# Spectral mixing and gated MLP on one core: the first eight chunks of the first matmul stage in another order, with the first four row norms on VectorE

## The chip, the cores and the metric

One core of a Trainium2 chip runs the whole kernel. Its engines are named as in the profile: PE (TensorE, matmuls), PEld (its weight loads), DVE (VectorE), ACT (ScalarE), POOL (GpSimd) and SP (SyncE, which here only issues DMAs). Each engine takes its own instructions strictly in the order in which the program gives them and waits on semaphores of the others. The metric is the device time of one execution in microseconds (us), as the median of several runs. A lower number is better.

## What is computed

The part that matters is the first block, an adaptive layer norm followed by a Fourier mixing over the sequence (2048 positions) and the hidden axis (512):

```python
sa, ca, ga, sb, cb, gb = (mod[:, 0], mod[:, 1], mod[:, 2], mod[:, 3], mod[:, 4], mod[:, 5])
h = _layernorm(x, axis=-1) * (1 + ca) + sa
a = jnp.einsum("bsd,ed->bse", h, dft_hid_re)
b = jnp.einsum("bsd,ed->bse", h, dft_hid_im)
y = jnp.einsum("ts,bse->bte", dft_seq_re, a) - jnp.einsum("ts,bse->bte", dft_seq_im, b)
x = x + ga * y
```

After it come a second layer norm, a gelu layer, a second sequence mixing with `w_sp`, a gate and an output projection. They are the other nine tenths of the time, and the change touches nothing in them.

## The kernel before

The sequence product is taken first, on the normalised rows, and the hidden transform later. Every float32 product is made of three matmuls on a high and a low part of each operand: high by high, high by low, low by high. The high part is a rounded copy (on ACT, line 249, or DVE, line 247), and the low part is the rest (a DVE subtraction, line 256).

**Rows.** `x` is cut into 16 row tiles of 128 positions. Row tile s is normed into `xn` (its column 0 is set to 1, a place for the mean), copied into a high part `hh` (line 416, ACT), and the rest goes into a low part `hl` (line 421, DVE). For rows 0 to 3 `stats_first` makes mean and variance on DVE (lines 374 to 377), then POOL raises the variance to the power -1/2 (line 378) and multiplies it with the negated mean (line 379). ACT then applies scale and shift (line 119). Rows 4 to 9 go the same way by `stats_x` and `norm` (lines 103 to 115), with three small POOL instructions each (lines 107, 108, 115) and a POOL memset of column 0 (line 402).

**Chunks.** The DFT matrices are loaded in blocks of 512 by 512 (1 MB, four DMAs of 256 KB each) into `stage`, a pool of two buffers. One chunk n is a quarter of a block, turned by a DVE transpose into `t` (line 176 for one chunk, line 220 for two), split into `ah` and `al`, and used in 12 matmuls: four column groups of the row tile, three products each. Below, "chunk n" is that group of 12 matmuls, "ah n" and "al n" its operands, and "row s" the row tile. `ah` has four buffers, `al` three, and `t` two buffers of two chunks each.

In the first output tile (t = 0) the real and imaginary products collect in PSUM banks 0 to 3 and 4 to 7. Before the change chunks 0 to 3 are the four quarters of real block 0 with rows 0 to 3, chunks 4 to 7 the four quarters of imaginary block 1 with the same rows, chunks 8 to 11 real block 2 with rows 4 to 7, chunks 12 to 15 imaginary block 3 with rows 4 to 7, and so on.

**Order.** Nothing is scheduled by a tool: the order on each engine is the order of the code. For each n the loop calls `prep(n)` (low part of chunk n + 2, transpose of chunks n + 4 and n + 5, high part of chunk n + 3), then `mm_a(n)` (the matmuls), then `run(n)`, which issues what `at(n, ...)` has put down for this place. The work before chunk 0 is written out by hand. A DMA issue waits, besides its buffer, for the DMA that was issued eight places earlier to land.

Of the kernel before, what the change touches and what calls it, by code (L numbers as in the profile page):

```python
# [13 lines left out]
P = 128  # L14
# [5 lines left out]
def fnet_gmlp_kernel(  # L20
# [181 lines left out]
    def turn_one(n):  # L202
        squares(slot(n), stage[n // 4], n % 4)
# [167 lines left out]
    def stats_first(s):  # L371

        m = spool.tile([P, 12], F32, tag="first", bufs=4, name=f"first{s}")
        nc.vector.bn_stats(m[:, :6], X[s])
        mv = m[:, 8:]
        nc.vector.bn_aggr(mv[:, :2], m[:, :6])
        nc.vector.tensor_scalar(mv[:, 1:2], mv[:, 1:2], EPS, None, op0=ALU.add)
        nc.gpsimd.tensor_tensor(mv[:, 2:3], mv[:, 1:2], mhalf, op=ALU.pow)
        nc.gpsimd.tensor_scalar(mv[:, 3:4], mv[:, 0:1], mv[:, 2:3], -1.0, op0=ALU.mult, op1=ALU.mult)
        NRM[s] = mv[:, 2:3], mv[:, 3:4]  # L380
# [48 lines left out]
    def mm_a(n):  # L429
        t, r = divmod(n, 8 * NQ)  # L430
        j, s = ((r // 4) % 2, r // 8 * 4 + r % 4) if t == 0 else (r // NS, r % NS)
# [5 lines left out]
        if n < 4:  # L437
            order = (h_hi[s], al), (h_lo[s], ah)
            for a, b in ((h_hi[s], ah),) + (order if n else order[::-1]):
                for k in range(ND):  # L440
                    nc.tensor.matmul(GP[0, 0, k], a[:, k, :], b, start=s == 0 and b is ah and a is h_hi[s], stop=False)
            return
# [505 lines left out]
    for s, n in ((4, 4), (5, 4), (6, 6), (7, 6), (8, 10), (9, 10)):  # L948
# [242 lines left out]
```

## Time and profile before

| | |
|---|---|
| median of 3 runs | 949.35 us (948.96 to 949.91) |
| profiled execution, whole | 948.98 us |
| profiled execution, span of the instructions | 947.2 us |
| PE busy | 940.0 us, 99% of the span |
| DVE busy | 704.0 us, 74% |
| ACT busy | 388.4 us, 41% |
| POOL busy | 174.3 us, 18% |
| PE share of the chain that ended last | 95% |

The profiled execution takes 1.8 us more than the span, which lies outside the instructions. PE is busy all the time but for 7.2 us, so a change shows in the time only where PE starts earlier, waits less, or waits more. PE's waits are listed by who ended them; the timeline then tells when each of them was and what came late.

### The profile page before, as it was taken

The page shows a single profiled execution, that of the slowest core. Times are in us where ns is not written, and L with a number is a line of the kernel's source. Part 1 is how long each engine was busy: PE and PEld are TensorE (multiplying, and loading weights), DVE is VectorE, ACT ScalarE, POOL GpSimd, SP SyncE. Part 2 cuts the span into 40 slices and gives each one's busy share as a digit, 9 for nine tenths or more (in the row PEclk, how much of TensorE's full clock was granted, in tenths as well). Part 3 has the DMA queues.
Part 4 walks back from the last instruction along what each step waited for, and adds up shares of the span by engine and source line. Part 5 has one row for each costly group of instructions (what it writes and reads, how often), then busy time and mean ns, then how long its engine had stood idle before and what let it go on. Part 6 is the DMA issues. An engine that isn't in the chain of part 4 may idle for free.

```text
span 947.2 us, 12274 instructions
## 1 busy us (share of the span) xinstructions
PE 940.0 (99%) x4160; PEld 781.3 (82%) x4160; DVE 704.0 (74%) x1039; ACT 388.4 (41%) x665; POOL 174.3 (18%) x331
## 2 busy tenths in 40 slices
PE   8999999999999999999999999999999999999998
PEld 5888888888888888888888999888888888888886
DVE  6799857775576667767978588877788688885872
ACT  4685424232132222322776356644544444331221
POOL 2430000221531144122332265200000000000000
PEclk9999999999999999999999999999999999999999
DMA  9996553576437975996397985555554456833541
GB/s 213 222 222 149 113 139 89 147 187 156 134 89 195 274 212 153 279 280 140 126 307 281 327 266 152 155 114 134 128 133 90 105 118 140 206 102 120 192 162 57
DMA packets 249230, 161.25 MB, mean 170 GB/s; under 512 B 130192, under 2 KB 218512, under 8 KB 249040
## 3 DMA queue, kind: packets, MB, share of 16 engines
q1 hardware_dynamic: 235792, 120.75, 52.8%
q0 software_dynamic: 11984, 39.07, 11.3%
q10 hardware_dynamic: 1392, 0.66, 0.3%
q8 instruction: 32, 0.52, 0.2%
q14 instruction: 30, 0.25, 0.1%
HBM read 123.73 MB, written 36.70 MB: 169 GB/s over the span
## 4 chain that ended last, share of the span: by engine, by line
PE 95%; DMA 2%; DVE 1%; ACT 1%; POOL 1%; issue 0%; ACTq 0%; SPq 0%; POOLq 0%; DVEq 0%
PE gp L95 12%; PE gp L96 12%; PE gp L97 12%; PE gw L96 10%; PE gw L97 10%; PE gw L95 10%; PE yp L96 3%; PE yp L95 3%; PE yp L97 3%; PE z2p L97 3%; PE z2p L96 3%; PE z2p L95 3%; PE op L96 3%; PE op L95 3%; PE op L97 3%; PE z1p L95 1%
## 5 line engine op out<-in xcount | busy, mean ns | idle before, releaser
L249 ACT ACTIVATE ah<-t 128x512 fp32r<-128x512 f32 x263 | 164.2, 627 | 306.6 <-PE gp L97 184.9
L256 DVE TENSOR_TENSOR al<-t,ah 128x512 fp32r<-128x512 f32 x264 | 180.1, 685 | 142.7 <-PE gp L96 65.3
L95 PE MATMUL gp<-ah,hh 128*128 128x512 f32 x496 | 192.9, 389 | 0.0
L96 PE MATMUL gp<-al,hh 128*128 128x512 f32 x496 | 192.9, 389 | 0.0
L97 PE MATMUL gp<-ah,hl 128*128 128x512 f32 x496 | 192.9, 389 | 0.0
L97 PE MATMUL gw<-ah,bl 128*128 128x512 f32 x400 | 155.6, 389 | 0.0
L96 PE MATMUL gw<-al,bh 128*128 128x512 f32 x400 | 155.6, 389 | 0.0
L95 PE MATMUL gw<-ah,bh 128*128 128x512 f32 x400 | 155.6, 389 | 0.0
L97 PEld LDWEIGHTS gp<-ah,hl 128*128 128x128 f32 x496 | 93.1, 188 | 19.4
L95 PEld LDWEIGHTS gp<-ah,hh 128*128 128x128 f32 x496 | 93.1, 188 | 19.3
L96 PEld LDWEIGHTS gp<-al,hh 128*128 128x128 f32 x496 | 93.1, 188 | 19.2
L95 PEld LDWEIGHTS gw<-ah,bh 128*128 128x128 f32 x400 | 75.1, 188 | 15.7
L97 PEld LDWEIGHTS gw<-ah,bl 128*128 128x128 f32 x400 | 75.1, 188 | 15.5
L96 PEld LDWEIGHTS gw<-al,bh 128*128 128x128 f32 x400 | 75.1, 188 | 15.5
L220 DVE STREAM_TRANSPOSE t<-stage 128x1024 f32<-128x1024 f32 x64 | 79.2, 1238 | 5.8 <-DMA stage<-in_A_dft_seq_re_dram 5.4
L214 DVE STREAM_TRANSPOSE t<-stage 128x1024 f32<-128x1024 f32 x56 | 69.3, 1238 | 0.0
L761 ACT ACTIVATE bh<-z 128x512 fp32r<-128x512 f32 (+1 forms) x56 | 32.8, 587 | 65.8 <-PE gw L96 65.8
L739 POOL DMA_DIRECT2D s_d<-sj x64 | 35.1, 550 | 110.5 <-DVE sj L731 81.5
L95 PE MATMUL yp<-hth,gh 128*128 128x512 f32 x128 | 49.8, 389 | 0.0
L96 PE MATMUL yp<-htl,gh 128*128 128x512 f32 x128 | 49.8, 389 | 0.0
L97 PE MATMUL yp<-hth,gl 128*128 128x512 f32 x128 | 49.8, 389 | 0.0
L96 PE MATMUL z2p<-wil,ah 128*128 128x448 f32 x128 | 46.7, 365 | 0.0
(204 smaller groups left out, 1419.3 us busy)
## 6 DMA issues: line engine op xcount, KB each, us to landing
stage<-in_A_dft_seq_im_dram SPq DMA_DIRECT2D x64, 256.0 KB, 5.5
sj<-in_B_w_sp_dram SPq DMA_DIRECT2D x32, 512.0 KB, 8.3
s_d<-sj POOLq DMA_DIRECT2D x64, 256.0 KB, 4.3
stage<-s_d SPq DMA_DIRECT2D x128, 128.0 KB, 2.9
stage<-in_A_dft_seq_re_dram SPq DMA_DIRECT2D x60, 256.0 KB, 5.3
stage<-in_B_w_sp_dram SPq DMA_DIRECT2D x96, 128.0 KB, 3.2
stage<-h_d SPq DMA_DIRECT2D x32, 256.0 KB, 6.0
wm<-in_w_mod_dram SPq DMA_DIRECT2D x16, 256.0 KB, 4.8
```

The lines of the kernel that those rows point to most:

```text
L95: nc.tensor.matmul(acc, ah, bh, start=first, stop=False, skip_group_check=go_on)
L96: nc.tensor.matmul(acc, ah, bl, start=False, stop=False, skip_group_check=go_on)
L97: nc.tensor.matmul(acc, al, bh, start=False, stop=last, skip_group_check=go_on)
L214: nc.vector.transpose(t.rearrange("p r (b i) -> p r b i", i=32), st[:, :, :, 16 * k:16 * k + 32])
L220: nc.vector.transpose(t.rearrange("p k (b i) -> p k b i", i=32), st[:, :, 32 * k:32 * k + 64].rearrange("p b (k i) -> p k b i", k=2))
L249: nc.scalar.activation(AH[n], source(n), AF.Copy)
L256: nc.vector.tensor_tensor(AL[n], source(n), AH[n].bitcast(F32), op=ALU.subtract)
L739: nc.gpsimd.dma_start(s_d[m, r, g][b * P:(b + 1) * P, :], a)
L761: nc.scalar.activation(BH[p, k][:, :w], b_of(p, k), AF.Copy)
```

## The change

Five things are changed, all before or in the first chunks:

- Chunks 0 to 7 alternate: an even chunk is a quarter of real block 0, an odd one the same quarter of imaginary block 1, both with the same row. So row s is used by chunks 2s and 2s + 1, where before chunks 0 to 3 used rows 0 to 3. Each of the eight chunks gets its own transpose of 512 columns (`turn_one`). All eight chunks run the matmuls product by product over the four column groups.
- Rows 0 to 3 are normed on DVE by one instruction (subtract the mean, multiply by the power, `norm_first`) and a DVE memset of column 0. POOL keeps the power alone, and ACT loses four norm instructions.
- The first halves of blocks 0 and 1 are loaded ahead of row 1, rows 1, 2 and 3 in loads of their own. Block 2 goes to the buffer `wb` of another pool, which is free at this time, so that it needn't wait for a `stage` buffer. Block 3 is loaded when chunk 7 has been turned.
- Chunk 0 is turned in two halves, and its high part is made in halves by ACT and DVE.
- The order after chunk 0 is written out: `prep(0)` to `prep(4)` are taken out, and what they did stands in a table. Rows 4 and 5, whose statistics stood together at chunk 4, are now made one after the other at chunks 4 and 5 and later.

The diff (empty lines left out):

```diff
--- before.py
+++ after.py
@@ -199,8 +199,15 @@
             T[n], T[n + 1] = t[:, 0, :], t[:, 1, :]
         return T[n]
-    def turn_one(n):
-        squares(slot(n), stage[n // 4], n % 4)
+    def turn_one(n, b0=0, b1=16):
+        if b0 == 0:
+            slot(n)
+        squares(T[n][:, 32 * b0:32 * b1], stage[n % 2][:, b0:b1], n // 2)
+        if n // 2 == 3 and b1 == 16:
+            stage.pop(n % 2)
+            if n % 2:
+                load(3)
     def turn_two(n):
@@ -376,8 +383,7 @@
         nc.vector.bn_aggr(mv[:, :2], m[:, :6])
         nc.vector.tensor_scalar(mv[:, 1:2], mv[:, 1:2], EPS, None, op0=ALU.add)
         nc.gpsimd.tensor_tensor(mv[:, 2:3], mv[:, 1:2], mhalf, op=ALU.pow)
-        nc.gpsimd.tensor_scalar(mv[:, 3:4], mv[:, 0:1], mv[:, 2:3], -1.0, op0=ALU.mult, op1=ALU.mult)
-        NRM[s] = mv[:, 2:3], mv[:, 3:4]
+        NRM[s] = mv[:, 0:1], mv[:, 2:3]
     def sum_x(s):
@@ -428,17 +434,17 @@
     def mm_a(n):
         t, r = divmod(n, 8 * NQ)
-        j, s = ((r // 4) % 2, r // 8 * 4 + r % 4) if t == 0 else (r // NS, r % NS)
+        j, s = (r % 2, r // 2) if n < 8 else ((r // 4) % 2, r // 8 * 4 + r % 4) if t == 0 else (r // NS, r % NS)
         if s == 0:
             for k in range(ND):
                 GP[t, j, k] = bank(4 * j + k if t == 0 else ring[0] % 6, f"gp{t}_{j}_{k}")
                 ring[0] += t > 0
         ah, al = AH.pop(n), AL.pop(n)
-        if n < 4:
+        if n < 8:
             order = (h_hi[s], al), (h_lo[s], ah)
-            for a, b in ((h_hi[s], ah),) + (order if n else order[::-1]):
+            for a, b in ((h_hi[s], ah),) + (order if j == 0 else order[::-1]):
                 for k in range(ND):
-                    nc.tensor.matmul(GP[0, 0, k], a[:, k, :], b, start=s == 0 and b is ah and a is h_hi[s], stop=False)
+                    nc.tensor.matmul(GP[0, j, k], a[:, k, :], b, start=s == 0 and b is ah and a is h_hi[s], stop=False)
             return
         for k in range(ND):
             matmul3(GP[t, j, k], h_hi[s][:, k, :], h_lo[s][:, k, :], ah, al, s == 0, s == NS - 1)
@@ -894,48 +900,69 @@
     both = (nc.sync, nc.scalar)
+    for b in range(2):
+        stage[b] = blocks.tile([P, 16, P], F32, tag="stage", bufs=2, name=f"stage{b}")
     load_x(0, range(1), both)
-    stage[0] = blocks.tile([P, 16, P], F32, tag="stage", bufs=2, name="stage0")
     load_block(stage[0], src[0], 0, P // 2, both)
-    load_x(0, range(1, 2), both)
+    load_block(stage[1], src[1], 0, P // 2, both)
+    load_x(0, range(1, 2))
     nc.scalar.activation(sc, ones[:, :ND], AF.Silu)
-    load_x(0, range(2, 4))
+    load_x(0, range(2, 3))
     load_block(stage[0], src[0], P // 2, P)
-    load(1)
+    load_block(stage[1], src[1], P // 2, P)
+    load_x(0, range(3, 4))
     load_x(1, range(2))
+    stage[2] = spool.tile([P, 16, P], F32, tag="wb", bufs=1, name="stage2")
+    load_block(stage[2], src[2])
     keep_busy(4, 5)
-    for s in range(4):
+    def norm_first(s):
         LN[s] = spool.tile([P, D], F32, tag="xn", bufs=4, name=f"xn{s}")
-        nc.gpsimd.memset(LN[s][:, 0:1], 1.0)
+        m = NRM.pop(s)
+        nc.vector.tensor_scalar(LN[s], X.pop(s), m[0], m[1], op0=ALU.subtract, op1=ALU.mult)
+        nc.vector.memset(LN[s][:, 0:1], 1.0)
+    def hi_half(n, b0, b1, eng=None):
+        if b0 == 0:
+            split_done.add((n, 0))
+            AH[n] = blocks.tile([P, Q], F32R, tag="ah", bufs=4, name=f"ah{n}")
+        c = slice(32 * b0, 32 * b1)
+        if eng:
+            eng.tensor_scalar(AH[n][:, c], T[n][:, c], 1.0, None, op0=ALU.mult)
+        else:
+            nc.scalar.activation(AH[n][:, c], T[n][:, c], AF.Copy)
     stats_first(0)
-    norm_x(0)
+    norm_first(0)
     hi_h(0)
-    turn_one(0)
-    prep_hi(0, nc.vector)
-    stats_first(1)
+    turn_one(0, 0, 8)
+    hi_half(0, 0, 8)
+    turn_one(0, 8, 16)
+    hi_half(0, 8, 16, nc.vector)
+    prep_lo(0)
     lo_h(0)
-    prep_lo(0)
-    norm_x(1)
-    hi_h(1)
     turn_one(1)
     prep_hi(1)
-    stats_first(2)
+    stats_first(1)
     prep_lo(1)
-    lo_h(1)
-    norm_x(2)
-    hi_h(2)
     turn_one(2)
     prep_hi(2)
-    stats_first(3)
-    turn_one(3)
-    prep_hi(3)
-    norm_x(3)
-    hi_h(3)
-    stage.pop(0)
-    load(2)
-    at(0, lo_h, 2)
-    at(0, turn_two, 4)
-    at(1, lo_h, 3)
+    norm_first(1)
+    hi_h(1)
+    prep_lo(2)
+    lo_h(1)
+    prepared.update(range(5))
+    for n, *todo in ((0, (turn_one, 3), (prep_hi, 3), (stats_first, 2), (prep_lo, 3), (turn_one, 4), (prep_hi, 4)),
+                     (1, (norm_first, 2), (hi_h, 2), (prep_lo, 4), (lo_h, 2), (turn_one, 5), (prep_hi, 5)),
+                     (2, (stats_first, 3), (prep_lo, 5), (turn_one, 6), (prep_hi, 6)),
+                     (3, (norm_first, 3), (hi_h, 3), (prep_lo, 6), (lo_h, 3), (turn_one, 7), (prep_hi, 7)),
+                     (4, (prep_lo, 7), (stats_x, 4), (turn_two, 8)),
+                     (5, (norm_x, 4), (hi_h, 4), (lo_h, 4), (stats_x, 5)),
+                     (6, (norm_x, 5), (hi_h, 5), (lo_h, 5))):
+        for f, *a in todo:
+            at(n, f, *a)
     at(0, load_x, 1, range(2, 4))
     at(2, load_row)
     at(9, silu_row)
@@ -945,7 +972,7 @@
     at(12, load_columns, 0)
     at(19, load_ht, 0)
     at(28, load_ht, 1)
-    for s, n in ((4, 4), (5, 4), (6, 6), (7, 6), (8, 10), (9, 10)):
+    for s, n in ((6, 6), (7, 6), (8, 10), (9, 10)):
         m = n + (s == 9)
         at(n, stats_x, s)
         at(m + 1, norm_x, s)
```

At the start DVE's instructions are these before the change, behind the statistics of row 0 (`first` is the statistics tile of a row, `t` a turned chunk; the number behind a name is the row or chunk, the one behind the underscore a running number):

```order
L176 STREAM_TRANSPOSE t0_187<-stage0_137 128x512
L247 TENSOR_SCALAR ah0_189<-t0_187 128x512
L374 BN_STATS first1_191<-x0_132 128x6
L376 BN_AGGR first1_191<-first1_191 128x2
L377 TENSOR_SCALAR first1_191<-first1_191 128x1
L421 TENSOR_TENSOR hl0_197<-xn0_170,hh0_185 128x512
L256 TENSOR_TENSOR al0_199<-t0_187,ah0_189 128x512
L176 STREAM_TRANSPOSE t0_187<-stage0_137 128x512
L374 BN_STATS first2_207<-x0_132 128x6
L376 BN_AGGR first2_207<-first2_207 128x2
L377 TENSOR_SCALAR first2_207<-first2_207 128x1
```

and these after it:

```order
L924 TENSOR_SCALAR xn0_188<-x0_134,first0_183 128x512
L925 MEMSET xn0_188 128x1
L176 STREAM_TRANSPOSE t0_193<-stage0_132 128x256 x2
L933 TENSOR_SCALAR ah0_195<-t0_193 128x256
L263 TENSOR_TENSOR al0_199<-t0_193,ah0_195 128x512
L427 TENSOR_TENSOR hl0_201<-xn0_188,hh0_191 128x512
L176 STREAM_TRANSPOSE t0_193<-stage1_133 128x512
L381 BN_STATS first1_206<-x0_134 128x6
L383 BN_AGGR first1_206<-first1_206 128x2
L384 TENSOR_SCALAR first1_206<-first1_206 128x1
L263 TENSOR_TENSOR al1_211<-t0_193,ah1_204 128x512
L176 STREAM_TRANSPOSE t2_213<-stage0_132 128x512
```

The row's norm (line 924) and memset now stand on DVE, where they stood on ACT and POOL; al0 stands ahead of hl0, and one row's work lies between the transposes of two chunks.

Around chunk 8, DVE has this before the change (`bstx` and `mvx` are the statistics of a row from 4 on; the first row below ends those of row 4, then come rows 5, 6 and 7):

```order
L105 BN_AGGR mvx_357<-bstx_355 128x2
L103 BN_STATS bstx_364<-x1_160 128x6
L105 BN_AGGR mvx_366<-bstx_364 128x2
L256 TENSOR_TENSOR al7_373<-t6_288,ah7_332 128x512
L256 TENSOR_TENSOR al8_400<-t8_330,ah8_375 128x512
L220 STREAM_TRANSPOSE t10_402<-stage2_236 128x1024
L103 BN_STATS bstx_427<-x1_160 128x6
L105 BN_AGGR mvx_429<-bstx_427 128x2
L103 BN_STATS bstx_436<-x1_160 128x6
L105 BN_AGGR mvx_438<-bstx_436 128x2
L256 TENSOR_TENSOR al9_445<-t8_330,ah9_409 128x512
L421 TENSOR_TENSOR hl4_461<-xn4_394,hh4_423 128x512
```

and this after it, again from the end of row 4's statistics on:

```order
L105 BN_AGGR mvx_360<-bstx_358 128x2
L227 STREAM_TRANSPOSE t8_367<-stage2_173 128x1024
L427 TENSOR_TENSOR hl4_393<-xn4_388,hh4_391 128x512
L103 BN_STATS bstx_395<-x1_168 128x6
L105 BN_AGGR mvx_397<-bstx_395 128x2
L263 TENSOR_TENSOR al8_409<-t8_367,ah8_374 128x512
L227 STREAM_TRANSPOSE t10_411<-stage2_173 128x1024
L427 TENSOR_TENSOR hl5_437<-xn5_432,hh5_435 128x512
L103 BN_STATS bstx_439<-x1_168 128x6
L105 BN_AGGR mvx_441<-bstx_439 128x2
L103 BN_STATS bstx_448<-x1_168 128x6
L105 BN_AGGR mvx_450<-bstx_448 128x2
```

The statistics of row 5 stood right behind those of row 4, and hl4 (with hl5 behind it) stood behind al8 and al9. Now hl4 stands ahead of row 5's statistics and of al8, and hl5 ahead of the statistics of rows 6 and 7; al9 is the row behind the last one shown.

ACT has this at the same place before the change:

```order
L249 ACTIVATE ah8_375<-t8_330 128x512
L119 ACTIVATE xn4_394<-x1_160,nmrx_362,rsx_359 128x511
L119 ACTIVATE xn5_397<-x1_160,nmrx_371,rsx_368 128x511
L249 ACTIVATE ah9_409<-t8_330 128x512
L416 ACTIVATE hh4_423<-xn4_394 128x512
L416 ACTIVATE hh5_425<-xn5_397 128x512
```

and this after it:

```order
L256 ACTIVATE ah8_374<-t8_367 128x512
L119 ACTIVATE xn4_388<-x1_168,nmrx_365,rsx_362 128x511
L422 ACTIVATE hh4_391<-xn4_388 128x512
L256 ACTIVATE ah9_418<-t8_367 128x512
L119 ACTIVATE xn5_432<-x1_168,nmrx_402,rsx_399 128x511
L422 ACTIVATE hh5_435<-xn5_432 128x512
```

The norms of rows 4 and 5 (line 119) stood together; now the copy hh4 and ah9 stand between them.

## Rows read from the trace of the kernel before

**Rows 1.** The page, part 1: busy time of each engine.

```profile
PE 940.0 (99%) x4160; PEld 781.3 (82%) x4160; DVE 704.0 (74%) x1039; ACT 388.4 (41%) x665; POOL 174.3 (18%) x331
```

**Rows 2.** Waits of PE over the span: us in total, times, longest.

```profile
PE gp L441 <- ACT ah L249: 1.1, 2, 0.7
PE z1p L95 <- DVE z1k L677: 0.4, 1, 0.4
PE gp L441 <- DVE hl L421: 0.4, 1, 0.4
PE z1g L95 <- ACT z1k L669: 0.3, 1, 0.3
```

**Rows 3.** Timeline of PE, 7 to 22 us: start, duration, instructions, idle before.

```profile
7.71 1.15 PE L441 MATMUL gp<-ah,hh 128*128 128x512 f32 x4
...
12.05 1.19 PE L441 MATMUL gp<-ah,hh 128*128 128x512 f32 x4 [0.69 <-ACT ah L249]
...
21.20 0.39 PE L95 MATMUL gp<-ah,hh 128*128 128x512 f32 x1
...
21.88 0.39 PE L95 MATMUL gp<-ah,hh 128*128 128x512 f32 x1
```

**Rows 4.** Groups of instructions, 0 to 45 us: busy and mean ns of one.

```profile
L256 DVE TENSOR_TENSOR al<-t,ah 128x512 fp32r<-128x512 f32 x15 | 10.1, 680 | 3.7 <-PE gp L96 1.9 <-ACT ah L249 1.8
L249 ACT ACTIVATE ah<-t 128x512 fp32r<-128x512 f32 x15 | 9.1, 622 | 7.3 <-DVE t L220 4.6 <-PE gp L97 2.5 <-DVE t L176 0.2
L220 DVE STREAM_TRANSPOSE t<-stage 128x1024 f32<-128x1024 f32 x6 | 7.4, 1240 | 1.4 <-DMA stage<-in_A_dft_seq_re_dram 1.4
...
L119 ACT ACTIVATE xn<-x,nmrx,rsx 128x511 f32<-128x511 f32 x6 | 4.9, 812 | 4.3 <-POOL nmrx L115 2.1 <-POOL xn L402 1.5 <-DMA stage<-in_A_dft_seq_re_dram 0.7
...
L176 DVE STREAM_TRANSPOSE t<-stage 128x512 f32<-128x512 f32 x4 | 2.8, 706 | 1.4 <-DMA stage<-in_A_dft_seq_re_dram 1.4
...
L247 DVE TENSOR_SCALAR ah<-t 128x512 fp32r<-128x512 f32 x1 | 0.4, 426 | 0.0
```

**Rows 5.** Groups of instructions of DVE over the whole span.

```profile
L484 DVE TENSOR_SCALAR acc<-ht,col 128x512 f32<-128x512 f32 x2 | 1.0, 477 | 0.0
```

**Rows 6.** Timeline of DVE, 3 to 33 us.

```profile
3.92 0.69 DVE L374 BATCH_NORM_STATS2 first<-x 128x6 f32<-128x512 f32 x1 [2.53 <-DMA x<-in_A_x_dram]
...
4.86 0.15 DVE L377 TENSOR_SCALAR first<-first 128x1 f32<-128x1 f32 x1
6.39 0.71 DVE L176 STREAM_TRANSPOSE t<-stage 128x512 f32<-128x512 f32 x1 [1.38 <-DMA stage<-in_A_dft_seq_re_dram]
...
25.60 0.18 DVE L105 BATCH_NORM_AGGREGATE mvx<-bstx 128x2 f32<-128x6 f32 x1
25.70 0.66 DVE L103 BATCH_NORM_STATS2 bstx<-x 128x6 f32<-128x512 f32 x1
...
26.50 1.29 DVE L256 TENSOR_TENSOR al<-t,ah 128x512 fp32r<-128x512 f32 x2
27.71 1.24 DVE L220 STREAM_TRANSPOSE t<-stage 128x1024 f32<-128x1024 f32 x1
```

**Rows 7.** Where an x load was issued at 6.2 to 6.6 us, and time to landing.

```profile
L364 SPq DMA_DIRECT2D x<-in_A_x_dram x2: 325/375/425, 6.2 to 6.6; - x2
...
DMA to landing us min/median/max: 2.5/2.6/2.7
```

**Rows 8.** Timeline of POOL, 25 to 30 us.

```profile
26.80 1.04 POOL L115 TENSOR_SCALAR nmrx<-mvx,rsx 128x1 f32<-128x1 f32 x1
...
28.85 0.26 POOL L115 TENSOR_SCALAR nmrx<-mvx,rsx 128x1 f32<-128x1 f32 x1
```

**Rows 9.** Timeline of ACT, 29 to 33 us.

```profile
30.39 1.14 ACT L416 ACTIVATE hh<-xn 128x512 fp32r<-128x512 f32 x2
```

**Rows 10.** Timeline of PE's weight loads, 5 to 7 us.

```profile
5.94 0.34 PEld L337 LDWEIGHTS busyp<-busy,ones 128*128 128x128 f32 x1 [0.52 <-issue]
6.73 0.19 PEld L337 LDWEIGHTS busyp<-busy,ones 128*128 128x128 f32 x1 [0.45 <-issue]
```

## The prediction, made before the changed kernel was run

> **What bounds the kernel now.** I read the busy times first: PE is busy for 940.0 of 947.2 us [rows 1], so only PE's idle time can be won, and new idle time is lost in full unless something later takes it up. Next, PE's waits: after the busy matmuls at the start they are five, and three of them lie in the first chunks, on ah and hl [rows 2]. The timeline of PE gives their price. In steady state three matmuls take 0.68 us (21.20 to 21.88), so a chunk of 12 takes 2.72 us. Chunks 0 to 3 run from 7.71 to 21.20, 13.49 us, where four chunks need 10.88 [rows 3]. So 2.6 us is what the start could give back. From 21.20 us on PE has no gap until the z stages, whose two waits [rows 2] the change doesn't touch; chunk 12 thus starts at 21.20 + 8 x 2.72 = 42.96 us before the change. Everything below is measured against this one time: from chunk 12 on, the order of the code is the same in both kernels.
>
> **What ends the waits now.** Between two chunks a whole row has to go through DVE (1.09 us of statistics from 3.92 to 5.01 [rows 6]), POOL, ACT (norm, hh) and DVE again (hl), beside transpose, ah and al. A chunk needs more of that than the 2.72 us that PE takes for it.
>
> **Alternating chunks (gain).** Now a row serves two chunks. Per pair DVE has: two transposes of 0.71, two al and one hl of 0.68 [rows 4], statistics 1.09, and the norm. The norm on DVE isn't in the trace. The nearest rows are a one-scalar instruction over the same 512 columns, 0.43 us [rows 4], and one with a scalar per partition, 0.48 us [rows 5]; an upper bound is the two-operand 0.68. I take 0.43, and 0.09 for the memset of one column (bound: the 0.15 of another one-column instruction [rows 6]). The sum is 5.07 us. Independent neighbours on DVE overlap by about 0.1 us (two al in 1.29, and the transpose starts at 27.71, 0.08 ahead of their end [rows 6]); six such joins give back 0.6. Waits of 0.3 us, mostly for ah behind its transpose, come on top. That is a period of 4.75 us for two chunks, for which PE needs 5.44. So DVE draws ahead of PE and the stalls of chunks 0 to 3 go.
>
> **The start itself (no gain).** Chunk 0 hangs on the first half block, which DVE gets at 6.39 [rows 6] as before, since the same loads stand ahead of it. Two half transposes at 0.44 (between 0.71 for 512 and 1.24 for 1024 columns [rows 4]; at least 0.35 each), with DVE's half of ah (0.43 at most, I take 0.29), end at 7.5; ACT's half runs beside. Before, transpose and ah ended at 7.56. PE starts at 7.65 instead of 7.71. The norm of row 0 no longer passes through ACT, so hh0 is there half a microsecond sooner, but hh0 isn't what is late. al0 is there at 8.2 and hl0 at 8.8, and PE asks for them at 8.6 and 9.5: no wait.
>
> **The loads.** Ahead of row 1 now stand the half of block 1 instead of rows 2 and 3: the same 1.5 MB as before up to the last of them, which landed at 6.6 + 2.7 = 9.3 us [rows 7]. With 0.1 to 0.2 us from landing to start, DVE gets row 1 at 9.4 to 9.5, just when the transpose of chunk 1 ends (9.4). Eight more DMAs stand on SP's queue; what is behind them (rows 4 and 5, block 2, block 3) is asked for at 25 us and later, and I count nothing. Block 2 in the other buffer no longer waits for chunk 3's transpose. Block 3 waits for chunk 6's, at about 21 us, as late as its issue was before, and its first transpose comes at about 37 us.
>
> So rows 1, 2 and 3 get their statistics at 9.4, 14.15 and 18.9 us, chunk 2 finds hh1 at 12.9 when PE asks at 13.1, and chunks 0 to 7 run without a gap: chunk 8 could start at 7.65 + 8 x 2.72 = 29.4 us, where it was 32.08. That is the gain, 2.65 us.
>
> **Rows 4 to 7 (loss).** Before, the statistics of rows 4 and 5 stood together and were done at 26.6, and hh4 and hh5 at 31.5 [rows 9], for chunks 8 and 9 at 32.1 and 34.8: half a microsecond of slack, with DVE never waiting for them, since al8, al9 and the next statistics stood ahead of hl4. Now hl4 stands ahead of row 5's statistics and of al8. Step by step:
> - From 18.9 DVE makes row 3's statistics, al5, chunk 6's transpose, the norm, al6, hl3 and chunk 7's transpose, until 23.7; ah7 takes ACT until 24.35 (0.62 [rows 4]); al7 ends at 25.1. Row 4's statistics are done at 25.9.
> - POOL's three instructions took 2.05 us from the end of row 4's statistics at 25.8 to 27.84 [rows 6, 8]; the last of them was 1.04 beside al7 and al8, and 0.26 for the next row at 28.85. Without that delay it is 1.3. Here a 1024-column transpose runs beside them, so 1.3: 27.2. ACT has ah8 first (27.7), then the norm (0.81), 28.4, and hh4, 29.05 [rows 4]. DVE has been idle since 27.0. hl4 ends at 29.75, row 5's statistics at 30.55, al8 at 31.15.
> - Chunk 8 starts at 29.4, and its second matmul, at 29.65, needs al8: it waits until 31.2, **1.55 us**. The chunk ends at 33.8.
> - Row 5 from 30.55: POOL loses 0.4 to al8 and ends at 32.25, norm 33.1, hh5 33.75, hl5 34.5, then the statistics of rows 6 and 7 until 36.05, and al9 at 36.65. Chunk 9's second matmul waits from 34.2 to 36.7, **2.5 us**; the chunk ends at 39.3.
> - Row 6's statistics are done at 35.3 and row 7's at 36.05. POOL has both by 38.3, ACT makes both norms and ah11 (39.7) before hh6 (40.25); hl6 behind al11 ends at 41.0. Chunk 10 waits from 39.3 to 40.3 for hh6 and **0.25** more for hl6: together **1.3 us**. It runs free from 41.1 and ends at 43.45; chunk 12 starts at 46.2.
>
> With some 0.1 us for each restart, the stalls are 5.9 us against the 2.65 won. **Sum:** chunk 12 at 46.2 instead of 42.96, +3.25 us. Nothing later takes that up or adds to it: block 4 and rows 8 on are needed at chunk 16, eleven microseconds later, and PE had no gap there before. From the profiled execution's 948.98 that is 952.2; the median lies 0.37 above it, so I forecast 952.6 us.
>
> [...] The same POOL instruction took 1.04 us beside two subtractions of DVE (26.80) and 0.26 beside a transpose (28.85) [rows 6, 8]. [...]
>
> **Bounds.** If POOL takes 2.05 us for a row instead of 1.3, row 4 loses little behind ah8, row 5 0.4 more, rows 6 and 7 0.4 to 0.8: up to +1.2. If row 1 lands half a microsecond later, all of the chain moves by it, +0.5; norms of 0.68 give +0.4. On the other side each of some 35 DVE instructions from 6.39 to 25.1 might overlap a little more; 0.05 each is -1.7. So 950.8 to 954.8.
>
> **Rivals.**
> - *Rows 4 to 7 are not late (faster).* The start is won and the chain is hidden, as it was before the change. It decides at al8: it must be there by 29.65, al9 by 32.4 and hl6 by 35.3, each over a microsecond ahead of the earliest sum above, so the row chain would have to go by another order than the one that I read. Then 2.65 us are won: 946.7. For it: only that rows 0 to 3 leave POOL and ACT emptier. Chance 0.06.
> - *Half of it (no change).* DVE is at row 4 some 1.7 us sooner, the whole chain moves with it, and the loss is 1.5: 950.8. Chance 0.11.
> - *PE's clock falls in the new gaps (slower still).* [...] Chance 0.10. [...]
> - *The start doesn't get better:* row 1 or block 1 lands 2 us later than by equal bytes. Chunk 1 or 2 stalls, but the chain behind sets the end: about 954. Within the forecast's chance.
>
> **How the numbers follow.** Forecast 0.73, with its bounds; clock 0.10; half 0.11; faster 0.06. What a measurement of this kernel can tell from no change is about 0.2%, 1.9 us: under 947.45 is faster, over 951.25 slower. So faster 0.06, same 0.11, slower 0.83, and the range of 950.8 to 954.8 leaves out the faster rival and the far ends.
>
> **What would show it.** In the profile after: no PE idle between 7.7 and 29.4; then three waits of PE on al (chunks 8 and 9) and on hh or hl (chunk 10), 1.5, 2.5 and 1.3 us; DVE idle for some 2 us ahead of hl4 and 1.5 ahead of hl5, ended by hh; the 2.72 us pace again from 46.2 us. I am wrong if chunk 8's second matmul starts before 30 us, or if PE's gaps lie elsewhere.

## The result and the profile after

| | before | after |
|---|---|---|
| median | 949.28 us (948.96 to 949.91, 6 runs) | 953.43 us (953.37 to 953.97, 6 runs) |
| profiled execution, span | 947.2 us | 951.7 us |
| start of chunk 8 | 32.08 us | 30.03 us |
| start of chunk 12 | 42.96 us | 47.44 us |

The ratio is 1.0046, with a 95% interval of 1.0036 to 1.0057: slower, by 4.2 us. Busy time of the changed kernel, in the page's first part:

```profile
PE 941.7 (99%) x4160; PEld 782.3 (82%) x4160; DVE 706.7 (74%) x1050; ACT 386.2 (41%) x662; POOL 171.1 (18%) x323
```

Its waits of PE (us in total, times, longest):

```profile
PE gp L96 <- DVE al L263: 4.0, 2, 2.4
...
PE gp L95 <- ACT hh L422: 0.2, 1, 0.2
```

The three waits of [rows 2] on ah and hl in the first chunks are gone, and two long ones on al stand in their place. PE's timeline after shows where (start, duration, instructions, idle before):

```profile
7.74 1.16 PE L447 MATMUL gp<-ah,hh 128*128 128x512 f32 x4
...
26.95 1.07 PE L447 MATMUL gp<-ah,hh 128*128 128x512 f32 x4
...
30.03 0.50 PE L95 MATMUL gp<-ah,hh 128*128 128x512 f32 x1 [0.20 <-ACT hh L422]
32.16 0.50 PE L96 MATMUL gp<-al,hh 128*128 128x512 f32 x1 [1.62 <-DVE al L263]
...
34.83 0.46 PE L95 MATMUL gp<-ah,hh 128*128 128x512 f32 x1
37.70 0.79 PE L96 MATMUL gp<-al,hh 128*128 128x512 f32 x1 [2.41 <-DVE al L263]
38.29 0.63 PE L97 MATMUL gp<-ah,hl 128*128 128x512 f32 x1
38.72 0.63 PE L95 MATMUL gp<-ah,hh 128*128 128x512 f32 x1
...
40.82 0.40 PE L97 MATMUL gp<-ah,hl 128*128 128x512 f32 x1
...
41.75 0.40 PE L95 MATMUL gp<-ah,hh 128*128 128x512 f32 x1
41.98 0.39 PE L96 MATMUL gp<-al,hh 128*128 128x512 f32 x1
42.33 0.50 PE L97 MATMUL gp<-ah,hl 128*128 128x512 f32 x1
...
47.44 0.39 PE L95 MATMUL gp<-ah,hh 128*128 128x512 f32 x1
```

Before the change, chunks 8 and 12 began here (PE's timeline before):

```profile
32.08 0.39 PE L95 MATMUL gp<-ah,hh 128*128 128x512 f32 x1
...
42.96 0.39 PE L95 MATMUL gp<-ah,hh 128*128 128x512 f32 x1
```

After it, chunk 7 begins at 26.95 us, with no gap since chunk 0 at 7.74, so chunk 8 could have begun 2.72 us later, at 29.67, 2.41 us ahead of before. That much the start wins. Chunks 7 to 11 then take 0.36, 2.08, 4.20, 0.25 and 0 us more than 2.72 each, 6.89 in all, and 6.89 - 2.41 is the 4.48 us by which chunk 12 is late. The difference of the spans is 4.5 us: nothing later adds or takes.

DVE's timeline after shows the order that the prediction read (statistics at line 103, al at 263, hl at 427, transpose at 227), with the two waits of DVE for hh4 and hh5:

```profile
25.66 0.69 DVE L103 BATCH_NORM_STATS2 bstx<-x 128x6 f32<-128x512 f32 x1
...
26.56 1.25 DVE L227 STREAM_TRANSPOSE t<-stage 128x1024 f32<-128x1024 f32 x1
30.01 0.69 DVE L427 TENSOR_TENSOR hl<-xn,hh 128x512 fp32r<-128x512 f32 x1 [2.21 <-ACT hh L422]
30.62 0.69 DVE L103 BATCH_NORM_STATS2 bstx<-x 128x6 f32<-128x512 f32 x1
...
31.44 0.66 DVE L263 TENSOR_TENSOR al<-t,ah 128x512 fp32r<-128x512 f32 x1
...
34.76 0.69 DVE L427 TENSOR_TENSOR hl<-xn,hh 128x512 fp32r<-128x512 f32 x1 [1.51 <-ACT hh L422]
...
36.99 1.26 DVE L263 TENSOR_TENSOR al<-t,ah 128x512 fp32r<-128x512 f32 x2
```

And ACT makes hh6 and hh7 in one pair, which end at 41.46 and 41.98 us (ACT's timeline after):

```profile
40.85 1.14 ACT L422 ACTIVATE hh<-xn 128x512 fp32r<-128x512 f32 x2
```

Before, this pair was done at 36.20 us (ACT's timeline before):

```profile
35.06 1.14 ACT L416 ACTIVATE hh<-xn 128x512 fp32r<-128x512 f32 x2
```

### The profile page after: what moved, and what is told of

It reads as the page before. It is cut to its first block, busy times and chain, and to the rows that moved or that the text cites. A ratio compares the mean times of both kernels' runs of the same rounds, so it can differ in the third digit from the quotient of the medians.

```text
span 951.7 us, 12278 instructions
## 1 busy us (share of the span) xinstructions
PE 941.7 (99%) x4160; PEld 782.3 (82%) x4160; DVE 706.7 (74%) x1050; ACT 386.2 (41%) x662; POOL 171.1 (18%) x323
## 4 chain that ended last, share of the span: by engine, by line
PE 93%; DMA 2%; SPq 1%; DVE 1%; ACT 1%; issue 1%; POOL 0%; ACTq 0%; DVEq 0%
PE gp L96 11%; PE gp L97 11%; PE gp L95 11%; PE gw L97 10%; PE gw L95 10%; PE gw L96 10%; PE yp L95 3%; PE yp L97 3%; PE yp L96 3%; PE z2p L95 3%; PE z2p L96 3%; PE z2p L97 3%; PE op L97 3%; PE op L96 3%; PE op L95 3%; PE z1p L95 1%
## 5 line engine op out<-in xcount | busy, mean ns | idle before, releaser
L96 PE MATMUL gp<-al,hh 128*128 128x512 f32 x480 | 187.7, 391 | 4.0 <-DVE al L263 4.0
L95 PE MATMUL gp<-ah,hh 128*128 128x512 f32 x480 | 187.4, 390 | 0.2 <-ACT hh L422 0.2
L97 PE MATMUL gp<-ah,hl 128*128 128x512 f32 x480 | 187.4, 390 | 0.0
L96 PEld LDWEIGHTS gp<-al,hh 128*128 128x128 f32 x480 | 90.5, 188 | 23.4 <-DVE al L263 4.7
L95 PEld LDWEIGHTS gp<-ah,hh 128*128 128x128 f32 x480 | 90.4, 188 | 19.6 <-ACT hh L422 0.9
L97 PEld LDWEIGHTS gp<-ah,hl 128*128 128x128 f32 x480 | 90.5, 189 | 19.1 <-DVE hl L427 0.4
L227 DVE STREAM_TRANSPOSE t<-stage 128x1024 f32<-128x1024 f32 x62 | 76.8, 1238 | 0.8 <-DMA stage<-in_A_dft_seq_re_dram 0.8
L221 DVE STREAM_TRANSPOSE t<-stage 128x1024 f32<-128x1024 f32 x56 | 69.4, 1238 | 0.1
```

Of the source, the lines that this page charges most:

```text
L95: nc.tensor.matmul(acc, ah, bh, start=first, stop=False, skip_group_check=go_on)
L96: nc.tensor.matmul(acc, ah, bl, start=False, stop=False, skip_group_check=go_on)
L97: nc.tensor.matmul(acc, al, bh, start=False, stop=last, skip_group_check=go_on)
L221: nc.vector.transpose(t.rearrange("p r (b i) -> p r b i", i=32), st[:, :, :, 16 * k:16 * k + 32])
L227: nc.vector.transpose(t.rearrange("p k (b i) -> p k b i", i=32), st[:, :, 32 * k:32 * k + 64].rearrange("p b (k i) -> p k b i", k=2))
```

## The experiments

The theory: the start is won, and the loss is the order of rows 4 to 7, no more. Its rivals: the load of the new norm on DVE, the clock in the gaps, and a limit behind the rows that would keep the gain away in any order. Each run has its own runs of the kernel before beside it, 949.0 to 949.2 us in all of them.

**Rows 4 to 7 where they were (e2).** On top of the changed kernel:

```diff
-                     (4, (prep_lo, 7), (stats_x, 4), (turn_two, 8)),
-                     (5, (norm_x, 4), (hi_h, 4), (lo_h, 4), (stats_x, 5)),
-                     (6, (norm_x, 5), (hi_h, 5), (lo_h, 5))):
+                     (4, (prep_lo, 7), (turn_two, 8))):
-    for s, n in ((6, 6), (7, 6), (8, 10), (9, 10)):
+    for s, n in ((4, 4), (5, 4), (6, 6), (7, 6), (8, 10), (9, 10)):
```

> The changed kernel with the work on rows 4 to 7 at the places that it had before the change (statistics of 4 and 5 together at chunk 4, of 6 and 7 at chunk 6, hl4 and hl5 behind al9). Theory: DVE is one transpose period later at this place than in the kernel before, so hh4 comes at about 32.5 and hl4 at about 35; chunk 8 starts 3 us late and waits once more for hl4, but chunks 9 to 11 run through; chunk 12 at 43.9 us, the time 3 to 3.5 us under the changed kernel, about 950. Rival (only the waits for al8 and al9 cost, rows 4 and 5 are no matter): chunk 12 at 40.5, 946.5.

Measured: 951.33 us (950.04 to 951.52), ratio 1.0022 (1.0012 to 1.0031), chunk 12 at 45.29. PE's timeline has one long gap, ahead of chunk 8:

```profile
32.51 0.50 PE L95 MATMUL gp<-ah,hh 128*128 128x512 f32 x1 [2.77 <-ACT hh L422]
...
33.91 0.63 PE L95 MATMUL gp<-ah,hh 128*128 128x512 f32 x1
```

So the old place of the rows isn't good for the new start either: hh4 and hh5 are made from 31.84 us on, 1.45 later than before [rows 9], while PE wants them 2.4 us sooner. The gap is 2.8 us, and behind it the matmuls come 0.43 us apart instead of 0.23 until 36.04 (the mean granted clock is 0.76 from 29.4 to 36.5 us), where nothing waits that would hide it. Chunk 8 begins 0.43 us later than before the change, and chunk 12 2.33 later: most of the 1.9 us between is this slow stretch, which the expectation (chunk 12 at 43.9) had left out. The one execution of the nine with a mean granted clock of 1.000 took 950.04 us; the others had 0.998.

**Row 5's statistics back beside row 4's (e3).**

```diff
-                     (4, (prep_lo, 7), (stats_x, 4), (turn_two, 8)),
-                     (5, (norm_x, 4), (hi_h, 4), (lo_h, 4), (stats_x, 5)),
+                     (4, (prep_lo, 7), (stats_x, 4), (stats_x, 5), (turn_two, 8)),
+                     (5, (norm_x, 4), (hi_h, 4), (lo_h, 4)),
```

> The changed kernel with one step moved: row 5's statistics stand beside row 4's, as before the change, ahead of block 2's transpose and of hl4; hh5, hl5 and rows 6 and 7 stay where the change has them. Theory (the wait for hh4 in front of hl4, with row 5's statistics behind it, makes chunk 9 late): xn5 no longer waits for row 5's statistics at 31.5, hh5 follows hh4 on ScalarE at about 31, hl5 behind al8 and block 2's second transpose or before, chunk 9's wait falls from 2.41 us to 0.7 or less and chunk 10's wait stays at about the same moment, so chunk 12 begins some 1.5 us sooner, at 45.9, and the time is 951.9. Rival (rows 6 and 7 alone set the end, at hh6 41.46 and hl6 42.27): chunk 12 stays at 47.4, 953.4 us.

Measured: 951.88 us (951.72 to 952.41), ratio 1.0029 (1.0018 to 1.0040), chunk 12 at 45.68 us. Chunk 9 waits for nothing. hh6 ends at 39.71 instead of 41.46 us, 1.75 sooner, and chunk 10 begins when it is there:

```profile
39.77 0.50 PE L95 MATMUL gp<-ah,hh 128*128 128x512 f32 x1 [0.60 <-ACT hh L422]
```

Chunk 12 moved by 1.76 us, as much as hh6 did. The place of this one step, behind DVE's wait for hh4, makes 1.6 of the 4.2 us. It also shows that the waits don't add up: chunk 8's and 9's lie ahead of hh6, which alone decides when chunk 10 begins.

**All of rows 4 to 7 by hand (e1).** The statistics of rows 4, 5 and 6 stand one chunk sooner, and every hl stands behind an al that needn't wait (al7 ahead of hl4, al8 ahead of hl5). The rows taken out and row 3's unchanged steps are left out here:

```diff
-    prepared.update(range(5))
+    prepared.update(range(10))
...
+                     (3, ..., (lo_h, 3), (stats_x, 4), (turn_one, 7), (prep_hi, 7), (norm_x, 4)),
+                     (4, (stats_x, 5), (prep_lo, 7), (hi_h, 4), (turn_two, 8), (prep_hi, 8), (norm_x, 5)),
+                     (5, (lo_h, 4), (prep_lo, 8), (stats_x, 6), (hi_h, 5), (prep_hi, 9), (norm_x, 6)),
+                     (6, (lo_h, 5), (prep_lo, 9), (turn_two, 10), (stats_x, 7), (hi_h, 6), (prep_hi, 10), (norm_x, 7)),
+                     (7, (lo_h, 6), (prep_lo, 10), (turn_two, 12), (hi_h, 7), (prep_hi, 11)),
+                     (8, (lo_h, 7), (prep_lo, 11), (prep_hi, 12))):
...
-    for s, n in ((6, 6), (7, 6), (8, 10), (9, 10)):
+    for s, n in ((8, 10), (9, 10)):
```

> The changed kernel with only the work on rows 4 to 7 in another order: row 4's statistics ahead of chunk 7's transpose, row 5's ahead of al7, each row's norm and memset ahead of the next row's statistics on POOL, and al8 and al9 ahead of the next statistics on DVE. Theory (the loss is only this order on DVE, ACT and POOL): PE has no gap from chunk 0 to chunk 12, chunk 12 starts at 40.5 us instead of 47.4, and the time is 7 us shorter than the changed kernel, 946.5, that is 2.5 under the kernel before. Rival (the new chunk order and the norm on DVE load DVE so much that chunks 8 to 11 are late in any order): al8 or hl5 still later than chunk 8 or 9, chunk 12 at 43 or later, 949 or more.

Measured: 950.64 us (948.32 to 951.33), ratio 1.0013 (1.0004 to 1.0022). Chunk 12 begins at 40.54 us, without a gap since 7.76: all of the 6.9 us are the order of rows 4 to 7, and the start keeps its 2.4 us. But the time isn't under before, since at chunk 15 stands a new wait. PE's timeline:

```profile
48.70 0.39 PE L95 MATMUL gp<-ah,hh 128*128 128x512 f32 x1
50.64 0.50 PE L96 MATMUL gp<-al,hh 128*128 128x512 f32 x1 [1.55 <-DVE al L263]
```

And DVE's, which shows what al15 stands behind:

```profile
47.41 1.25 DVE L227 STREAM_TRANSPOSE t<-stage 128x1024 f32<-128x1024 f32 x1 [5.06 <-DMA stage<-in_A_dft_seq_re_dram]
48.58 0.67 DVE L176 STREAM_TRANSPOSE wt<-wb 128x512 f32<-128x512 f32 x1
49.29 0.69 DVE L328 TENSOR_TENSOR wt<-wt,crow 128x512 f32<-128x512 f32 x1
49.90 0.69 DVE L263 TENSOR_TENSOR al<-t,ah 128x512 fp32r<-128x512 f32 x1
```

DVE sits idle for 5 us at the first transpose of block 4, which landed at 47.29, as it had before the change (47.28). Between this transpose and al15 stands a second cause: a step on wb1 (`weigh_column`, lines 176 and 328). Without it al15 would be done some 1.3 us sooner, and most of this wait would be gone. The landing isn't fixed either: in the changed kernel, with the same order of loads, block 4 landed at 48.87. Chunk 16 begins at 53.27 us, 0.57 ahead of before instead of 2.42. In 6 of the 11 executions the mean granted clock was 0.998 and the span 948.9 to 949.6 us, in 5 it was 1.000 and 946.5 to 948.2; the profiled one is of the latter. The next run shows what a fallen clock behind such a gap costs.

**Block 4's loads ahead of wb1's (e6).** On top of e1; the first two steps on wb1 move back as well:

```diff
-    at(5, load_columns, 1)
+    at(7, load_columns, 1)
-    for j, ns in ((1, (12, 14, 17, 18)), (0, (21, 22, 23, 24))):
+    for j, ns in ((1, (15, 16, 17, 18)), (0, (21, 22, 23, 24))):
```

> The kernel of the run e1_rows_by_hand, in which chunk 12 began at 40.54 us but chunk 15's second matmul waited 1.94 us on al15, with two changes: the four loads of wb1 are issued behind those of block 4 (both are 1 MB and SP's queue issues in order), and the four steps that transpose and weigh wb1 stand at chunks 15 to 18 instead of 12, 14, 17 and 18. Theory (the loads are the next bound: al15 stands on VectorE behind block 4's first transpose, which waited 5.06 us until block 4 had landed at 47.29): block 4 now lands when wb1 did, at about 43.0, its transpose starts at 43.1 to 43.5, and al15 is there long before 48.7. No PE gap between 7.7 us and chunk 16, which begins at 51.4 instead of 53.84 before the change and 53.27 in e1: 946.6 to 947.2 us, 2 to 2.5 under the kernel before. Rival (al15 was late because VectorE has too much to do there, with the load only part of it): a wait stays at chunk 15 or comes back at chunks 16 to 19, where block 5 lands at about 57, and the time is that of e1, 948.5 to 950.6.

Measured: 950.43 us (948.62 to 951.54), ratio 1.0009 (1.0000 to 1.0018). Theory and rival were each right in part. The wait at chunk 15 is gone and chunk 16 begins at 51.57 us, but block 5 is now the late one, and steps on wb1 stand between its transpose and al19. DVE's timeline:

```profile
59.21 1.25 DVE L227 STREAM_TRANSPOSE t<-stage 128x1024 f32<-128x1024 f32 x1 [4.89 <-DMA stage<-in_A_dft_seq_im_dram]
...
60.95 0.70 DVE L176 STREAM_TRANSPOSE wt<-wb 128x512 f32<-128x512 f32 x1
61.68 0.69 DVE L328 TENSOR_TENSOR wt<-wt,crow 128x512 f32<-128x512 f32 x1
62.29 0.68 DVE L263 TENSOR_TENSOR al<-t,ah 128x512 fp32r<-128x512 f32 x1
```

PE's at chunk 19:

```profile
59.73 0.39 PE L95 MATMUL gp<-ah,hh 128*128 128x512 f32 x1
63.03 0.50 PE L96 MATMUL gp<-al,hh 128*128 128x512 f32 x1 [2.92 <-DVE al L263]
...
64.45 0.63 PE L95 MATMUL gp<-ah,hh 128*128 128x512 f32 x1
```

From 64.06 to 67.44 us the matmuls come 0.43 us apart instead of 0.23, some eight of them: 1.6 us on top of the wait (the mean granted clock is 0.78 from 59.7 to 67.5 us). Block 5 landed at 59.09 us here and at 55.90 in e1, with the same loads ahead of it: behind block 3, 1 MB took 4.7 us here and 4.3 in e1. So much of this wait can be the pace of the loads in this execution and not their order.

**Loads in the order of need (e8).** On top of e1, rows 12 to 15 and block 5 are issued ahead of wb1, and block 6 ahead of wb0; the steps on wb1 and wb0 on DVE come later with them:

```diff
-    at(5, load_columns, 1)
+    at(11, load_columns, 1)
-    at(12, load_columns, 0)
-    at(19, load_ht, 0)
+    at(15, load_columns, 0)
+    at(21, load_ht, 0)
-    for j, ns in ((1, (12, 14, 17, 18)), (0, (21, 22, 23, 24))):
+    for j, ns in ((1, (18, 19, 20, 21)), (0, (22, 23, 24, 24))):
-    at(20, scale_columns)
+    at(23, scale_columns)
```

> The kernel of the run e1_rows_by_hand (rows 4 to 7 by hand, no gap up to chunk 15) with the loads in the order in which their data are needed: rows 12 to 15 and block 5 stand ahead of wb1, block 6 ahead of wb0, and the steps that use wb1 and wb0 are 3 to 6 and 1 or 2 chunks later. In e6, where wb1 had only changed places with block 4, the wait had moved from block 4 (al15) to block 5 (its transpose at 59.21, al19, 2.9 us). Theory (each 1 MB load takes 4.5 us, and the blocks come late only because loads that nobody needs yet stand ahead of them): block 4 lands at 43 to 45, block 5 at 53 to 54.5, block 6 at 62 to 64, for the transposes that chunks 16, 20 and 24 need at 51, 62 and 73. No PE gap from 7.8 us up to the z stages; chunk 16 at 51.4 to 51.6 us, 2.3 us ahead of before, and so to the end: 946.8 to 947.2 us, granted clock 1.00. Rival (the loads as a whole are too slow for this start, whatever their order): a wait of 1 us or more on al at a chunk from 16 to 32, 948.5 us or more.

Measured: **946.76 us (946.39 to 947.17), ratio 0.9975 (0.9965 to 0.9985)**, 2.4 us under before and 6.7 under the changed kernel: this version beats both. Behind the busy matmuls PE's waits are only the two of the z stages in [rows 2]:

```profile
PE busyp L344 <- DVE busy L284: 1.5, 1, 1.5
PE z1p L95 <- DVE z1k L683: 0.4, 1, 0.4
PE z1g L95 <- ACT z1k L675: 0.3, 1, 0.3
```

Block 5 has landed at 54.45 us instead of 59.09 (e6), and its transpose costs DVE half a microsecond of waiting (DVE's timeline):

```profile
54.63 1.25 DVE L227 STREAM_TRANSPOSE t<-stage 128x1024 f32<-128x1024 f32 x1 [0.45 <-DMA stage<-in_A_dft_seq_im_dram]
```

In the profiled execution chunk 16 begins at 51.96 us, 1.9 ahead of before but not at the expected 51.4 to 51.6: chunk 0 begins only at 8.28, since its half block landed later. (In the other profiled kernels with this start it begins between 7.60 and 8.00.) The loads and the steps on wb1 were moved together, in e6 and here; which of the two takes how much of the wait away wasn't tried apart.

**The same load order in the kernel before (e10).** The same lines as in e8's diff, on the kernel before.

> The kernel before with nothing but the load order of e8_blocks_first (rows 12 to 15 and block 5 ahead of wb1, block 6 ahead of wb0, the steps on wb1 and wb0 later). Theory (before the change the stalls of chunks 0 to 3 set the end and the loads came just in time behind them, so their order alone is worth nothing): chunk 16 at 53.84 as before, 949.0 to 949.5 us. Rival (the load order by itself is what gains in e8): 947 us.

Measured: 949.14 us (948.91 to 949.84), ratio 1.0000 (0.9991 to 1.0009), chunk 16 at 54.07 behind a chunk 0 at 7.92. The load order, with the steps that go with it, is worth nothing without the faster start, and the faster start nothing without it (e1).

**Rows 0 to 3 normed on ACT again (e4).**

```diff
-        NRM[s] = mv[:, 0:1], mv[:, 2:3]
+        nc.gpsimd.tensor_scalar(mv[:, 3:4], mv[:, 0:1], mv[:, 2:3], -1.0, op0=ALU.mult, op1=ALU.mult)
+        NRM[s] = mv[:, 2:3], mv[:, 3:4]
...
-        nc.vector.tensor_scalar(LN[s], X.pop(s), m[0], m[1], op0=ALU.subtract, op1=ALU.mult)
-        nc.vector.memset(LN[s][:, 0:1], 1.0)
+        nc.gpsimd.memset(LN[s][:, 0:1], 1.0)
+        norm_x(s)
```

> The changed kernel with the norm of rows 0 to 3 back on ACT and POOL (power and shift on POOL, scale and shift on ACT, memset on POOL); all other parts of the change stay. Theory (the norm on DVE shortens the chain from statistics to hh, which matters more than the DVE time that it takes): chunk 2 waits 0.8 us for hh1, chunks 4 and 6 little, DVE is 1 to 3 us later at row 4, and all the later stalls stay; chunk 12 at 48.5 to 50, the time 1 to 2.6 us over the changed kernel. Rival (DVE's load is what makes rows 4 to 7 late): 0.55 us less of it in each pair of chunks brings row 4 forward by 1.5 us, and the time falls by about that.

Measured: 956.03 us (955.97 to 956.31), ratio 1.0074 (1.0061 to 1.0088). The norm on DVE helps by 2.6 us. Without it hh1 is late (PE's timeline), each pair of chunks takes 5.7 us, and row 4 begins 2.5 us later on DVE (28.21 instead of 25.66):

```profile
14.09 1.20 PE L448 MATMUL gp<-ah,hh 128*128 128x512 f32 x4 [0.47 <-ACT hh L423]
...
34.68 0.80 PE L96 MATMUL gp<-al,hh 128*128 128x512 f32 x1 [1.63 <-DVE al L263]
```

**The two small parts undone (e7).** Chunk 0's high part whole again on DVE, and block 2 in a `stage` buffer:

```diff
-            if n % 2:
-                load(3)
+            load(2 + n % 2)
...
-    stage[2] = spool.tile([P, 16, P], F32, tag="wb", bufs=1, name="stage2")
-    load_block(stage[2], src[2])
...
-    turn_one(0, 0, 8)
-    hi_half(0, 0, 8)
-    turn_one(0, 8, 16)
-    hi_half(0, 8, 16, nc.vector)
+    turn_one(0)
+    prep_hi(0, nc.vector)
```

> The changed kernel without its two small parts: chunk 0's hi part is again one transpose and one product on VectorE (no halves on two engines), and block 2 takes a buffer of the two again, so its loads wait for chunk 6's transpose (it began at 15.95 us and ends at 16.65; the loads were issued at 17.25 to 19.27). Theory: the halves start chunk 0 at most 0.1 us sooner, and block 2's loads move behind those of rows 6 and 7 by 2 us at most, landing at 26.7 instead of 25.56, where its transpose started at 26.56. So nothing moves at chunk 8 by more than 0.3 us: chunk 12 at 47.4 to 47.8, 953.4 to 953.8 us. Rival (the third buffer is needed): block 2 lands 2 us later and al8 with it, chunk 12 at 49 or later, 955.

Measured: 957.07 us (956.85 to 957.59), ratio 1.0083 (1.0070 to 1.0097). The rival was right. The expectation took chunk 4's transpose, at 15.95, for chunk 6's, which runs from 20.87 to 21.57 us. Block 2's loads thus start at 21.59 and land at 29.85, and DVE waits for them:

```profile
29.98 1.25 DVE L226 STREAM_TRANSPOSE t<-stage 128x1024 f32<-128x1024 f32 x1 [3.42 <-DMA stage<-in_A_dft_seq_re_dram]
```

Chunk 12 is 3.4 us later, the 3.42 of this wait: the buffer is worth nearly all of the 3.6 us. Chunk 0 begins at 7.82 instead of 7.74 us, with the first transpose at 6.50 in both; the halves are worth a tenth of a microsecond at most.

**The gaps filled with zeros (e5, e5b).** Matmuls by a tile of zeros stand in the gaps of chunks 8 and 9. In e5 the tile was made on ACT at chunk 6:

```diff
+            if n in (8, 9) and k == 0:
...
+                for _ in range({8: 6, 9: 10}[n]):
+                    nc.tensor.matmul(GP[t, j, k], zeros_r, ah, start=False, stop=False)
...
+    at(6, lambda: nc.scalar.activation(zeros_r, ones, AF.Copy, scale=0.0))
```

> The changed kernel with 6 more matmuls with zero weights behind the first matmul of chunk 8 and 10 behind that of chunk 9, so that PE isn't idle while it waits for al8 and al9 (they add zero to the sums). [...]

Measured: 957.78 us (957.37 to 958.18), ratio 1.0092. It tells nothing of the clock: the zeros stood behind hh5 on ACT, PE waited 4.45 us for them, until 35.05, and this was a new gap. In e5b they are made ahead of the first row:

> The changed kernel with matmuls by a tile of zeros in the two gaps of chunks 8 and 9 (6 behind chunk 8's first matmul, 10 behind chunk 9's), so that PE is not idle there; they add nothing to the sums. The zeros are made at the very start, ahead of the row chain, so that they are waited for by nobody. Theory (the half clock from 37.70 to 40.82 us is hidden, since hh6 came at 41.46 and PE had to wait for it): the granted clock stays at 1.00, PE waits for hh6 as long as the slow matmuls took before, chunk 12 begins at 47.2 to 47.5 us, 953.2 to 953.5. Rival (the fall of the clock is what made the stall longer than forecast): chunk 12 at about 46.4, 952.4 us.

Measured: 954.03 us (953.68 to 954.49), ratio 1.0051 (1.0037 to 1.0065). The window from 34.8 to 42.7 us (length, then busy time of PE, PEld, DVE, ACT and POOL, then PE's granted clock) in the changed kernel:

```profile
34.80:42.70 7.90, 5.49 (x17) 3.92 (x17) 6.26 (x11) 4.36 (x9) 2.81 (x8) 0.78 1.18 221
```

And in e5b:

```profile
34.80:42.70 7.90, 6.68 (x27) 4.41 (x27) 6.04 (x11) 4.37 (x9) 2.80 (x8) 1.00 1.18 225
```

The granted clock stays at 1.00, and PE then waits for hh6 instead:

```profile
41.77 0.50 PE L95 MATMUL gp<-ah,hh 128*128 128x512 f32 x1 [1.00 <-ACT hh L422]
```

Chunk 0 begins 0.26 us later here than in the changed kernel (8.00 and 7.74), and so does chunk 12 (47.70 and 47.44). The fall thus costs nothing in the changed kernel: counted from chunk 0, its slow matmuls let chunk 10 begin 0.24 us later, but the third matmul of chunk 10 has to wait for hl6 in both.

## Why the prediction was right, and where it wasn't

The forecast was 952.6 us, slower, by waits on al8, al9 and hh6 behind a start that is won. The sign, the time and the waits for al8 and al9 (1.62 and 2.41 us) came so, and e1 shows the mechanism: another order of rows 4 to 7 alone brings chunk 12 from 47.44 to 40.54 us. The third wait, 1.3 us at chunk 10, isn't in the profile as one: chunk 9's slow matmuls fill its place. By its steps:

| step | forecast | measured |
|---|---|---|
| chunk 0 starts | 7.65 us | 7.74 us |
| statistics of rows 1, 2, 3 start | 9.4, 14.15, 18.9 | 9.54, 14.36, 19.28 |
| chunk 8 could start | 29.4 | 29.67 |
| row 4's statistics done | 25.9 | 26.56 |
| hh4 done | 29.05 | 29.98 |
| al8 done | 31.15 | 32.10 |
| al9 done | 36.65 | 37.65 |
| hh6, hl6 done | 40.25, 41.0 | 41.46, 42.27 |
| chunk 12 starts | 46.2 | 47.44 |

- **The term that was mis-sized** is the row chain's way to row 4: 0.7 us short at its statistics and 0.9 at hh4, and this is carried to the end. Row 1's statistics start 0.14 us late, a pair of chunks took DVE 4.82 to 4.92 us instead of 4.75 (the norm 0.50 to 0.55 instead of 0.43), and from row 3's statistics to the end of chunk 7's transpose it was 4.99 instead of 4.8. The wait for ah7 ahead of al7, 0.78 us, was in the sum with 0.7. Behind hh4 the steps held to 0.35 us. The upper end of the range covered it. Chunk 12 is 1.24 us later than forecast and the time only 0.83, which is luck: the forecast had added 0.37 us from the profiled execution to the median, and after the change the two are 953.46 and 953.43.
- **POOL's delay** beside subtractions came as forecast for row 5 (its first instruction took 0.54 us beside al8, 0.18 for row 4) and was 0.7 us for row 6: its last instruction took 1.01 us beside al9 and al10, and 0.27 for row 7 (POOL's timeline):

```profile
37.28 1.01 POOL L115 TENSOR_SCALAR nmrx<-mvx,rsx 128x1 f32<-128x1 f32 x1
...
39.31 0.27 POOL L115 TENSOR_SCALAR nmrx<-mvx,rsx 128x1 f32<-128x1 f32 x1
```

 Row 6's last one ended at 38.29, just behind the second subtraction (36.99 + 1.26 = 38.25). In [rows 8] it ended at 27.84, and the second subtraction there at 27.79 (26.50 + 1.29 [rows 6]). What makes it wait isn't shown. Row 7's statistics were 1.0 us late already (37.07 instead of 36.05), so no more than some 0.2 of hh6's 1.2 us can lie here.
- **The rival on the clock** was right that the clock falls, and wrong that this makes the kernel slower still. It was the author's guess: before the change the mean granted clock is 1.00 in each stretch from 1.5 to 43.0 us. In chunk 9's wait it did fall: the mean is 0.78 in the window from 34.8 to 42.7 us and 0.50 from 37.7 to 40.7, after 1.00 from 29.4 to 34.8, with matmuls 0.43 us apart instead of 0.23. But the waits for hh6 and hl6 hide all of it (e5b), and what lies beyond the forecast is the row chain's. The forecast's sum has no term for the clock at all. That it needed none is luck of this order: in e2 and e6 nothing hides the fall, and it costs 1.6 us and more.
- **Wrong:** "Nothing later takes that up or adds to it: block 4 and rows 8 on are needed at chunk 16, eleven microseconds later". It holds in the changed kernel only because that kernel is late. al15 stands on DVE behind block 4's first transpose and a step on wb1, so block 4 is needed by chunk 15, and in the loads' order it landed at 47.29 (e1) to 48.87 us (the changed kernel). The rival "Rows 4 to 7 are not late", priced at 946.7 us, would thus have given what e1 gave, 948.3 to 951.3. The 946.7 of that sum is what e8 measured (946.76), with the loads in another order and the steps on them later.
- **Misread, without effect:** block 3's loads were issued at 24.27 us and not at 21, since SP waited for one of block 2's, eight places earlier. They landed at 34.77, ahead of block 3's first transpose at 38.16. And the slack of hh4 before the change was 1.1 us and not 0.5: 31.5 is the end of hh5, the second of the pair in [rows 9].
- **Missed:** the value of block 2's buffer. The text names the wait that it takes away and gives it no price; e7 measured 3.6 us, 3.4 of them by this wait. It is one of the conditions of the gain at the start.

## What to carry to other kernels

An engine that takes its instructions in order turns one early wait into a wait for all that stands behind it (here row 5's statistics behind DVE's wait of 2.21 us for hh4 made 1.6 of the 4.2 us, e3): put the statistics of the next rows, and the low parts that are due, ahead of a step that waits for another engine. When a start is sped up, look at once for the next deadline in the same order: here first the rows, then the loads and what stands behind them on DVE. The loads came just in time before, and 1 MB of them took 4.0 to 5.9 us of the queue, mostly 4.2 to 4.8 (from landing to landing in e1 and e8). Several waits in a row are not several prices; the last operand to arrive sets the end, and what lay ahead of hh6 and hl6 cost nothing here, be it idle time (e3) or a clock of 0.50 (e5b).

## What the runs showed of the hardware

The granted clock fell in or behind gaps that one length doesn't set apart. It fell after 2.41 us of waiting (the changed kernel, chunk 9: 0.50 from 37.7 to 40.7 us), after 2.77 (e2: a mean of 0.76 from 29.4 to 36.5) and 2.92 (e6: 0.78 from 59.7 to 67.5), and after 1.02 and 0.82 us with one matmul between them (e3: 0.76 from 29.4 to 36.5). Behind each of these the matmuls came 0.43 us apart for a while instead of 0.23. It held after a single 1.62 us (the changed kernel, chunk 8: 1.00 from 29.4 to 34.8) and 1.55 us (e1's profiled execution: 1.00 from 48 to 54). In e1 and e6 the mean clock was 0.997 or 0.998 in some executions and 0.999 or 1.000 in others of the same program, and the spans of these differ by some 2 us. Where the clock fell and nothing hid it, a gap of 2.9 us cost 1.6 us more than its length (e6), and one of 2.8 us 1.9 more (e2, with a short wait for hl4 in it).
